# Loading a projection with two rows per partition, weights with a stride, and another order of a set-up

## The chip, the cores and the metric

The kernel runs on one core of a Trainium2 chip. A core has a matrix engine (TensorE, PE in the profile; PEld are its weight loads), a vector engine (VectorE, DVE), a scalar engine (ScalarE, ACT), GpSimd (POOL) and SyncE (SP); the last two issue the DMA transfers here, GpSimd those that change the type. The engines run side by side and wait for each other by semaphores. The metric is the device time of one execution in microseconds (us); of several executions, the median.

## The reference

Longformer attention on 8 batches of 8 heads, 576 tokens and 64 channels, followed by a two-layer projection with a "snake" activation on 4608 tokens. Cut to what matters:

```python
# attention: window of +-32 tokens, plus 8 global tokens
scores = scale * q @ k.T
attn   = softmax(where(mask, scores, -1e9))
x      = (attn @ v), laid out as 4608 tokens x 512
# projection
h   = x @ w_in                       # 512 -> 2048 features
s   = sin(alpha * h)
g   = h + s * s / (alpha + 1e-9)     # alpha: one number per feature
out = g @ w_out                      # 2048 -> 512
```

All inputs and the output are float32; the products take bfloat16.

## The kernel before

All four big tensors of the projection live in SBUF: `w_in` as 128 partitions x 4 chunks x 2048 features, `w_out` as 128 partitions x 16 feature tiles x 512, and `alphaT`, `recipT` as 128 partitions x 16, one column per feature tile (`recipT` is 1/(alpha + 1e-9)). A feature tile `nt` is 128 features that stand on the 128 partitions of PSUM after the first product. Before, tile `nt` holds the features nt*128 to nt*128 + 127 in order.

The order of work is written out by hand; each engine runs its instructions in the order in which the program calls them. `attention(b)` does one batch in four pairs of heads `hp`: `scores` (L814) into the PSUM tiles ring, zn or zd, the exponential (L822), a mask `cover` (L831); `denominators` (products with ones, L862, into zd, their logarithm L on ScalarE, L772, and the sums GD of the global tokens, L756); `inverse` (R = exp(-L), L779); and the numerators (products with v, L862, and with the global values, L878) that `normalise` (L908) multiplies by R into `xT`, the input of the projection. `gemm1(b)` then forms the 16 feature tiles: 8 products each (L1115, 4 chunks by 2 halves of the columns, each with its own weight load), a sine and a square on ScalarE (L1162, L1165) or a square on VectorE (L1167), and the sum into H (L1168). The second product, `gemm2` (L1220), is a generator: `fill(n)` takes n of its products and puts them into TensorE's queue between the attention work of the next batch. The first call, `fill(START)` with START = 7, stands at the head of the attention of batch 1; two fills of 9 products follow.

Batch 0 has a set-up of its own, `first_batch`. No second product is there yet to fill in. At its end it forms denominators, inverses and numerators of the four pairs in an order written out there, and sets `alphaT` and `recipT` in `set_recip`: a transpose of `arow` by TensorE (L710), a copy (L711), an addition (L712) and a reciprocal (L713) on VectorE. `warm` (L569) issues products with ones whose result nobody reads.

The weights come by GpSimd's queue: `load_w_in(lo, hi)` (L426) loads a range of columns, `load_w_out(gs)` (L432) a range of rows, with the cast to bfloat16 on the way. On the same queue stand the loads of q and k of batches 0 and 1 (`load_lying`, L456), the cast of v and q into DRAM for later batches (L334), and the casts of the global keys and queries (`gkq`, L717). Every DMA of that queue first waits until the eighth DMA before it has landed.

`judge` at the end checks a bound on the arguments of the sine; it sums the squares of `w_in` per feature (L1060, 16 products of one column each) into 16 columns that must agree with those of `alphaT`.

## Time and profile before

| what | value |
|---|---|
| median of 3 runs | 339.67 us (337.75 to 339.68) |
| the profiled execution | 338.49 us |
| its span, first to last instruction | 336.8 us |
| TensorE busy | 316.2 us (94%) |
| VectorE busy | 255.9 us (76%) |
| ScalarE busy | 277.1 us (82%) |
| GpSimd busy | 143.7 us (43%) |

The shares are means over stages with different limits: the set-up of batch 0 (to about 28.6 us), the first product of batch 0 (to about 51 us), then for each further batch attention with the second product of the batch before beside it, and its first product. Lines of a view give an engine, the line of the kernel, the operation, what it writes and reads, and its times. An idle time in brackets is followed by what ended it; "issue" means that the profile shows nothing that the engine waited for.

### The profile page before, as it was taken

What the parts mean: (1) busy time and instruction counts of PE and PEld (TensorE: products, weight loads), DVE (VectorE), ACT (ScalarE), POOL (GpSimd) and SP (SyncE); (2) the same over time, 40 slices, a digit from 0 to 9 for tenths busy, and PEclk for the clock granted to TensorE, in tenths of its full rate; (3) what the DMA queues carried; (4) which work ended last, traced back from release to release, by engine and by line L of the source; (5) the groups of instructions that cost most, each with busy time, mean ns of one, the idle gap of its engine ahead of it and who ended that gap; (6) DMA issues with size and microseconds to landing.
All of it is one profiled execution on the core that took longest, in us unless ns stands there. A gap on an engine that the chain in (4) does not pass through costs nothing.

```text
span 336.8 us, 11878 instructions
## 1 busy us (share of the span) xinstructions
PE 316.2 (94%) x4812; PEld 202.8 (60%) x4812; DVE 255.9 (76%) x488; ACT 277.1 (82%) x402; POOL 143.7 (43%) x296
## 2 busy tenths in 40 slices
PE   0778999999999999999999999999999999999993
PEld 0765765577556765667556755676567745665553
DVE  4885896887887788688877788778868888788930
ACT  6775888989998889988998889889898898889611
POOL 7983324349516670666355652487060000004500
PEclk9999999999999999999999999999999999999998
DMA  7999999999989998999969993899999311010232
GB/s 104 114 162 205 186 226 169 152 166 135 181 143 133 190 124 137 94 119 186 151 93 137 172 162 85 131 176 136 132 111 133 65 60 42 1 33 8 73 93 69
DMA packets 141942, 42.01 MB, mean 125 GB/s; under 512 B 126426, under 2 KB 136794, under 8 KB 141882
## 3 DMA queue, kind: packets, MB, share of 16 engines
q0 software_dynamic: 100096, 18.51, 71.1%
q1 hardware_dynamic: 41786, 22.69, 34.1%
q8 instruction: 38, 0.62, 0.8%
q14 instruction: 22, 0.18, 0.2%
HBM read 41.95 MB, written 20.77 MB: 186 GB/s over the span
## 4 chain that ended last, share of the span: by engine, by line
PE 87%; DVE 4%; ACT 3%; issue 2%; DMA 1%; POOL 1%; DVEq 0%; POOLq 0%
PE zo L1220 38%; PE zn L1115 14%; PE zr L1115 11%; PE zd L1115 10%; PE ring L814 4%; PE zd L862 4%; PE zn L862 2%; DVE H L1168 2%; DMA g0k<-in_k_dram,grow 1%; ACT sb L1162 1%; PE zn L814 1%; PE zr L862 1%; DVE recipT L712 1%; DVE s L1167 1%; PE zo L630 1%
## 5 line engine op out<-in xcount | busy, mean ns | idle before, releaser
L1220 PE MATMUL zo<-w_out,H 128*128 128x512 bf16 (+1 forms) x576 | 147.1, 377 | 0.3 <-DVE KX L637 0.3
L1115 PEld LDWEIGHTS <-w_in 128*128 128x128 bf16 x1024 | 100.1, 98 | 43.9 <-issue 8.3
L1220 PEld LDWEIGHTS <-H 128*128 128x128 bf16 x592 | 53.7, 98 | 46.2 <-issue 0.4
L1115 PE MATMUL zn<-xT,w_in 128*128 128x288 bf16 (+1 forms) x384 | 57.7, 290 | 1.6 <-DVE H L1168 1.4
L1115 PE MATMUL zr<-xT,w_in 128*128 128x288 bf16 x320 | 48.0, 288 | 0.3
L1168 DVE SCALAR_TENSOR_TENSOR H<-s,recipT,zn 128x576 bf16<-128x576 bf16 (+1 forms) x48 | 39.4, 822 | 10.4 <-ACT s L1165 6.5
L1162 ACT ACTIVATE sb<-zn,alphaT 128x576 bf16<-128x576 f32 (+1 forms) x48 | 35.7, 743 | 13.7 <-PE zn L1115 13.2
L1115 PE MATMUL zd<-xT,w_in 128*128 128x288 bf16 x320 | 46.3, 288 | 0.3 <-DVE H L1168 0.2
L822 ACT ACTIVATE E<-ring 128x720 bf16<-128x720 f32 x46 | 35.9, 780 | 8.3 <-PE ring L814 7.7
L1167 DVE TENSOR_TENSOR s<-sb 128x576 bf16<-128x576 bf16 (+1 forms) x70 | 32.6, 465 | 12.2 <-ACT sb L1162 12.0
L1165 ACT ACTIVATE s<-sb 128x576 bf16<-128x576 bf16 (+1 forms) x58 | 40.0, 689 | 1.8
L831 DVE TENSOR_TENSOR E<-E,MASKT 128x720 bf16<-128x720 bf16 x64 | 33.5, 529 | 7.6 <-ACT E L822 5.6
L1168 DVE SCALAR_TENSOR_TENSOR H<-s,recipT,zd 128x576 bf16<-128x576 bf16 (+1 forms) x40 | 32.9, 822 | 7.6 <-ACT s L1165 5.0
L1168 DVE SCALAR_TENSOR_TENSOR H<-s,recipT,zr 128x576 bf16<-128x576 bf16 (+1 forms) x40 | 32.9, 822 | 6.6 <-ACT s L1165 5.0
L344 POOL DMA_DIRECT2D kd<-in_k_dram x48 | 31.4, 657 | 10.4 <-issue 8.0
L1162 ACT ACTIVATE sb<-zd,alphaT 128x576 bf16<-128x576 f32 (+1 forms) x40 | 29.6, 740 | 5.2 <-PE zd L1115 5.1
L1162 ACT ACTIVATE sb<-zr,alphaT 128x576 bf16<-128x576 f32 (+1 forms) x40 | 29.6, 740 | 4.3 <-PE zr L1115 4.3
L1210 POOL COPY H<-H 128x11 bf16 (+1 forms) x16 | 7.2, 453 | 57.6 <-DVE H L1168 56.7
L346 POOL DMA_DIRECT2D vd<-in_v_dram x48 | 30.5, 645 | 1.7 <-issue 1.3
L346 POOL DMA_DIRECT2D qd<-in_q_dram x40 | 25.4, 635 | 6.0 <-issue 6.0
L1227 ACT COPY osb<-zo 128x512 f32<-128x512 f32 (+1 forms) x33 | 19.1, 580 | 10.6 <-PE zo L1220 7.0
L814 PEld LDWEIGHTS <-KX 64*64 64x64 bf16 x896 | 15.8, 112 | 19.4 <-issue 19.0
(171 smaller groups left out, 377.7 us busy)
## 6 DMA issues: line engine op xcount, KB each, us to landing
VF<-vd SPq DMA_DIRECT2D x14, 336.0 KB
kd<-in_k_dram POOLq DMA_DIRECT2D x48, 72.0 KB, 4.8
vd<-in_v_dram POOLq DMA_DIRECT2D x48, 72.0 KB, 4.1
qd<-in_q_dram POOLq DMA_DIRECT2D x40, 72.0 KB, 5.5
w_out<-in_moe_w_out_dram POOLq DMA_DIRECT2D x2, 1024.0 KB, 25.7
out_dram<-osb SPq DMA_DIRECT2D x7, 256.0 KB
out_dram<-osb SPq DMA_DIRECT2D x8, 224.0 KB
out_dram<-osb SPq DMA_DIRECT2D x8, 192.0 KB
```

The costliest lines, as they stand in the source:

```text
L344: nc.gpsimd.dma_start(out=dst[:, :, h], in_=src.rearrange("(i a) d -> a i d", a=KT))
L346: nc.gpsimd.dma_start(out=dst[:, h], in_=src)
L814: nc.tensor.matmul(out=z[half * D : (half + 1) * D, t, 0 : G3 * WCOL].rearrange("p (m x c) -> p m x c", x=2, c=60)[:, m % G3, :, c0:c1], l ...
L822: nc.scalar.activation(out=weights(hp, g), in_=z[:, :, 0 : G3 * WCOL], func=AF.Exp, scale=scale)
L831: nc.vector.tensor_tensor(out=Eg, in0=Eg, in1=MASKT[:, None, G3 * g : G3 * (g + 1), :].rearrange("p o m c -> p o (m c)").to_broadcast([P, ...
L862: nc.tensor.matmul(out=nd(hp, key)[t * D : (t + 1) * D, half, :, a - half * CUT : z - half * CUT], lhsT=ones[rows, 0:D] if key else values ...
L1115: nc.tensor.matmul(out=h_part, lhsT=w_in[:, c, nt * P : (nt + 1) * P], rhs=xT[:, c, lo:hi], start=(c == 0), stop=(c == CT - 1), skip_group ...
L1162: nc.scalar.activation(out=sb[:, 0:W], in_=h, func=AF.Sin, scale=alphaT[:, nt : nt + 1])
L1165: nc.scalar.activation(out=s2[:, 0:W], in_=sb[:, 0:W], func=AF.Square)
L1167: nc.vector.tensor_tensor(out=s2[:, 0:W], in0=sb[:, 0:W], in1=sb[:, 0:W], op=ALU.mult)
L1168: nc.vector.scalar_tensor_tensor(out=H2[:, nt, r0 : r0 + W], in0=s2[:, 0:W], scalar=recipT[:, nt : nt + 1], in1=h, op0=ALU.mult, op1=ALU.add,)
L1220: nc.tensor.matmul(out=ops[:, cols], lhsT=H2[:, nt, blk * P : (blk + 1) * P], rhs=w_out[:, nt, cols], start=(nt == 0), stop=(nt == NT - 1) ...
```

## The change

Four things change together.

**w_out.** It is loaded in four loads of four feature tiles instead of two of eight. Within a load each partition gets two neighbouring rows of `w_out` at a time, 1024 numbers that are contiguous in DRAM, for the two tiles 2t and 2t + 1.

**The features of a tile.** So partition p of tile 2t + j now holds feature 256 t + 2 p + j. The first product takes its weights accordingly: 128 columns of `w_in` with a step of two, by the new function `feature(nt)`. The same holds for the products of `judge` and for `general_path`, which is in the program but not run on these inputs. `alphaT` comes from an `arow` of 8 x 256 by two transposes, each of every other column.

**w_in.** The three loads are of 256, 768 and 1024 columns instead of 512, 512 and 1024, since tiles 0 and 1 now lie in the first 256 columns.

**The order in `first_batch` and in the second product of batch 0.** `inverse(0)` stands before the denominators of pair 2; `alphaT` is set right after the first numerators, a `warm` is added behind it, and the last denominators come before the second numerators; `recipT` is set after the last `normalise`. In `gemm2(0)` the first two blocks are both advanced to 12 of their 16 feature tiles, four tiles at a time in turn, where before each went to 8 at once.

On VectorE, at the end of batch 0's set-up, before (xT is the input of the projection; GD and GN are sums of the global tokens; zr, zn, zd are PSUM tiles):

```order
L908 TENSOR_TENSOR xT<-zn,R 128x576
L756 TENSOR_REDUCE GN<-zn 128x2x4
L711 COPY alphaT<-zo_125 128x16
L712 TENSOR_SCALAR recipT<-alphaT 128x16
L713 RECIPROCAL recipT<-recipT 128x16
L756 TENSOR_REDUCE GD<-zd 128x2x4
L908 TENSOR_TENSOR xT<-zr,R 128x576
L756 TENSOR_REDUCE GN<-zr 128x2x4
L908 TENSOR_TENSOR xT<-zd,R 128x576
L756 TENSOR_REDUCE GN<-zd 128x2x4
```

And the same stretch of VectorE now:

```order
L718 COPY alphaT<-zo_125 128x2x8
L768 TENSOR_REDUCE GD<-zd 128x2x4
L920 TENSOR_TENSOR xT<-zn,R 128x576
L768 TENSOR_REDUCE GN<-zn 128x2x4
L920 TENSOR_TENSOR xT<-zr,R 128x576
L768 TENSOR_REDUCE GN<-zr 128x2x4
L920 TENSOR_TENSOR xT<-zd,R 128x576
L768 TENSOR_REDUCE GN<-zd 128x2x4
L724 TENSOR_SCALAR recipT<-alphaT 128x16
L725 RECIPROCAL recipT<-recipT 128x16
```

The two instructions of recipT moved from ahead of the last GD to behind the last xT, and GD and alphaT moved ahead of the second xT.

On ScalarE, from the last exponentials of batch 0 to the first sine, before (L is the logarithm of the denominators, R their inverse):

```order
L822 ACTIVATE E<-zn 128x2x360
L772 ACTIVATE L<-zd 128x576
L779 ACTIVATE R<-L,shift 128x576 x3
L772 ACTIVATE L<-zd 128x576
L779 ACTIVATE R<-L,shift 128x576
L957 ACT_TABLE_LOAD
```

And now:

```order
L834 ACTIVATE E<-zn 128x2x360
L791 ACTIVATE R<-L,shift 128x576
L784 ACTIVATE L<-zd 128x576
L791 ACTIVATE R<-L,shift 128x576
L784 ACTIVATE L<-zd 128x576
L791 ACTIVATE R<-L,shift 128x576 x2
L972 ACT_TABLE_LOAD
```

The first inverse moved ahead of the third logarithm, and the last logarithm ahead of the third inverse.

On GpSimd's queue, from the q and k loads of batch 1 to the loads of w_out, before, with the semaphores that each waits for (DMASW0 to 7 go round, one per DMA):

```order
L426 DMA w_in<-in_moe_w_in_dram 128x4x512 [waits DMASW3_49]
L456 DMA H_97<-in_k_dram 48x4x768 [waits DMASW4_49]
L456 DMA H_97<-in_q_dram 48x4x768 [waits DMASW5_49]
L426 DMA w_in<-in_moe_w_in_dram 128x4x1024 [waits DMASW6_49]
L456 DMA H_97<-in_k_dram 48x4x768 [waits DMASW7_49]
L456 DMA H_97<-in_q_dram 48x4x768 [waits DMASW0_49]
L937 COPY seen<-VF_91 1x1 [waits DVE_49,Pool_49]
L334 DMA vd<-in_v_dram 4608x1x64 [waits DMASW1_49]
L432 DMA w_out<-in_moe_w_out_dram 128x8x512 [waits DMASW2_49]
L432 DMA w_out<-in_moe_w_out_dram 128x8x512 [waits DMASW3_49]
```

And now:

```order
L431 DMA w_in<-in_moe_w_in_dram 128x4x768 [waits DMASW3_49]
L461 DMA H_97<-in_k_dram 48x4x768 [waits DMASW4_49]
L461 DMA H_97<-in_q_dram 48x4x768 [waits DMASW5_49]
L431 DMA w_in<-in_moe_w_in_dram 128x4x1024 [waits DMASW6_49]
L461 DMA H_97<-in_k_dram 48x4x768 [waits DMASW7_49]
L461 DMA H_97<-in_q_dram 48x4x768 [waits DMASW0_49]
L949 COPY seen<-VF_91 1x1 [waits DVE_49,Pool_49]
L339 DMA vd<-in_v_dram 4608x1x64 [waits DMASW1_49]
L437 DMA w_out<-in_moe_w_out_dram 128x2x1024 [waits DMASW2_49]
L437 DMA w_out<-in_moe_w_out_dram 128x2x1024 [waits DMASW3_49]
L437 DMA w_out<-in_moe_w_out_dram 128x2x1024 [waits DMASW4_49]
L437 DMA w_out<-in_moe_w_out_dram 128x2x1024 [waits DMASW5_49]
```

The third and the fourth load of w_out now wait for the first k and q loads of batch 1 (DMASW4 and DMASW5) to have landed.

The diff, without the same edit of the weights in `general_path`:

```diff
+def feature(nt):
+
+    return slice((nt // 2) * 2 * P + nt % 2, (nt // 2 + 1) * 2 * P, 2)
...
     def load_w_in(lo, hi):
         if lo < hi:
-            cols = slice(lo * DFF // 4, hi * DFF // 4)
+            cols = slice(lo * DFF // 8, hi * DFF // 8)
...
     def load_w_out(gs):
         for g in gs:
             nc.gpsimd.dma_start(
-                out=w_out[:, 8 * g : 8 * g + 8, :],
-                in_=moe_w_out[8 * g * P : (8 * g + 8) * P, :].rearrange("(t p) n -> p t n", p=P),
+                out=w_out[:, 4 * g : 4 * g + 4, :].rearrange("p (t j) n -> p t (j n)", j=2),
+                in_=moe_w_out[4 * g * P : (4 * g + 4) * P, :].rearrange("(t p j) n -> p t (j n)", p=P, j=2),
             )
...
-    arow = setup.tile([NT, P], DT.float32, name="arow")
+    arow = setup.tile([NT // 2, 2 * P], DT.float32, name="arow")
...
-    nc.sync.dma_start(out=arow[:], in_=moe_alpha.rearrange("(t p) -> t p", p=P))
+    nc.sync.dma_start(out=arow[:], in_=moe_alpha.rearrange("(t p) -> t p", p=2 * P))
...
+    def set_alpha():
+        n = NT // 2
+        for j in range(2):
+            nc.tensor.transpose(out=zo[0][:, j * n : (j + 1) * n], in_=arow[:, j::2], identity=idf[0:n, 0:n])
+        nc.vector.tensor_copy(
+            out=alphaT[:].rearrange("p (t j) -> p j t", j=2),
+            in_=zo[0][:, 0:NT].rearrange("p (j t) -> p j t", j=2),
+        )
+
     def set_recip():
-        nc.tensor.transpose(out=zo[0][:, 0:NT], in_=arow[:], identity=idf[0:NT, 0:NT])
-        nc.vector.tensor_copy(out=alphaT[:], in_=zo[0][:, 0:NT])
         nc.vector.tensor_scalar(out=recipT[:], in0=alphaT[:], scalar1=1e-9, scalar2=None, op0=ALU.add)
         nc.vector.reciprocal(out=recipT[:], in_=recipT[:])
...
-                    load_w_in(1, 2)
+                    load_w_in(1, 4)
...
-                            load_w_in(2, 4)
+                            load_w_in(4, 8)
...
-                    load_w_out((0, 1))
+                    load_w_out(range(4))
                 beside(hp)
                 for g in range(2 * (hp > 0)):
                     cover(hp, g)
+                if hp == last:
+                    inverse(0)
                 if hp:
                     denominators(hp - 1)
             release_ring()
-            for hp in range(2):
-                inverse(hp)
-                first_numerators(hp)
-            set_recip()
-            inverse(last - 1)
+            inverse(1)
+            first_numerators(0)
+            set_alpha()
+            warm(zo[1], 1)
             denominators(last)
-            first_numerators(last - 1)
+            inverse(2)
+            first_numerators(1)
+            first_numerators(2)
             warm(zo[1], 1)
             products(last, 0)
...
             normalise(last)
+            set_recip()
...
-                out=zn[:, 0, nt : nt + 1], lhsT=W2[:, nt * P : (nt + 1) * P], rhs=ones[:, 0:1],
+                out=zn[:, 0, nt : nt + 1], lhsT=W2[:, feature(nt)], rhs=ones[:, 0:1],
...
-                        out=h_part, lhsT=w_in[:, c, nt * P : (nt + 1) * P], rhs=xT[:, c, lo:hi],
+                        out=h_part, lhsT=w_in[:, c, feature(nt)], rhs=xT[:, c, lo:hi],
...
-        ahead = {0: NT // 2, B - 1: SOON}.get(b, 0)
-        for blk in (lo, lo + 1):
-            yield from products(blk, bank(blk), range(ahead), full)
+        ahead = {0: 3 * NT // 4, B - 1: SOON}.get(b, 0)
+        step = NT // 4 if b == 0 else NT
+        for nt in range(0, ahead, step):
+            for blk in (lo, lo + 1):
+                yield from products(blk, bank(blk), range(nt, min(nt + step, ahead)), full)
```

More of the change, by code (lines that the diff above doesn't have):

```diff
@@ L201, in general_path @@
                         nc.tensor.matmul(
-                            out=hg[:, e, 0:HALF], lhsT=w_in[:, c, nt * P : (nt + 1) * P],
+                            out=hg[:, e, 0:HALF], lhsT=w_in[:, c, feature(nt)],
                             rhs=xT[:, c, e * HALF : (e + 1) * HALF],
```

## The prediction

> **What bounds the kernel now.** I read the busy time of each engine by stretches first, then the chain of work that ended last from 18 to 36 us, then the timeline around it. The first view gives a stretch, its length, and the busy time of TensorE, its weight loads, VectorE, ScalarE and GpSimd, each with its instruction count; below it stands one row of the timeline (start, length, engine, line, what it does, idle time before it):
>
> ```profile
> 0.00:50.00 50.00, 35.54 (x914) 27.21 (x915) 37.01 (x91) 37.02 (x55) 29.52 (x52) 1.00 1.23 165
> 50.00:310.00 260.00, 259.06 (x3746) 163.52 (x3746) 206.49 (x374) 230.32 (x337) 108.07 (x235) 1.00 1.11 122
> ...
> 6.51 0.24 PE L630 MATMUL zn<-identb,H 48*64 48x48 bf16 x1 [6.51 <-DMA H<-in_k_dram]
> ```
>
> TensorE is busy 259.06 of 260 us in the middle: there nothing but its own work counts, and a time won at the front arrives at the end undiminished. In the first 50 us it idles 50 - 35.54 = 14.5 us. All that a new order of the set-up can win lies in there. Of that, 6.51 us is the wait for the first load, which this change leaves alone. The chain (start, length, engine and line) shows what set the pace just before the product with w_in begins:
>
> ```profile
> 24.23 2.14 DVE recipT L712
> ...
> 26.40 0.25 DVE recipT L713
> 26.65 0.09 DVE GD L756
> ...
> 28.80 1.44 PE zn L1115 x6
> 30.24 0.93 PE zr L1115 x6
> ```
>
> recipT, 16 columns wide, takes 2.14 us, and behind it on VectorE stands the reduction GD, which must read zd before TensorE may write the last numerators into it. From the start of L712 to the GD piece are 26.65 - 24.23 = 2.42 us. The timeline tells why so small an instruction is so long:
>
> ```profile
> 23.79 2.16 POOL L334 DMA_DIRECT2D vd<-in_v_dram  x1
> 24.23 2.13 DVE L712 TENSOR_SCALAR recipT<-alphaT 128x16 f32<-128x16 f32 x1
> 24.38 0.51 PE L862 MATMUL zd<-E,ones 56*64 56x120 bf16 x16 [1.02 <-issue]
> 24.94 0.65 ACT L772 ACTIVATE L<-zd 128x576 f32<-128x576 f32 x1 [0.94 <-PE zd L862]
> 25.48 1.34 POOL L432 DMA_DIRECT2D w_out<-in_moe_w_out_dram  x1
> ```
>
> GpSimd is issuing the v load from 23.79 to 25.95, and L712 ends at 26.36. The reciprocal L713 of the same 16 columns takes 0.25 beside the next issue. I read it as one instruction held off by an issue that it happened to meet, with a work of its own of about 0.25.
>
> **1. The set-up of batch 0.** recipT moves behind the last normalise, alphaT ahead of the last denominators, and those ahead of the second numerators. Taking away L712 alone would not give 2.42: GD needs L, which ends at 24.94 + 0.65 = 25.59, so TensorE's zd could start near 25.7 in place of 26.78, 1.07 earlier. Moving the denominators forward puts L before that, and what is late next is TensorE's own queue. Its pieces:
>
> ```profile
> 20.24 0.79 PE L862 MATMUL zd<-E,ones 56*64 56x88 bf16 x28
> 20.86 0.77 PE L862 MATMUL zr<-E,VF 56*64 56x88 bf16 x28
> 21.68 0.78 PE L862 MATMUL zn<-E,VF 56*64 56x88 bf16 x28
> 22.66 0.28 PE L710 MATMUL zo<-idf,arow 16*128 16x16 f32 x1
> 24.67 0.82 PE L862 MATMUL zr<-E,VF 56*64 56x88 bf16 x28
> 25.69 0.61 PE L569 MATMUL zo<-ones 128*128 128x512 bf16 x1
> 26.78 0.79 PE L862 MATMUL zd<-E,VF 56*64 56x88 bf16 x28 [0.48 <-DVE GD L756]
> 27.77 1.03 PE L569 MATMUL zo<-ones 128*128 128x512 bf16 x2
> 28.60 1.65 PE L1115 MATMUL zn<-xT,w_in 128*128 128x288 bf16 x6
> ```
>
> From start to start: denominators 20.86 - 20.24 = 0.62, second numerators 22.66 - 21.68 = 0.98, third 25.69 - 24.67 = 1.02, last 27.77 - 26.78 = 0.99, the closing two warm-ups 28.60 - 27.77 = 0.83; and by their lengths, alpha 0.28 and one warm-up 0.61. The new queue behind the first numerators, from 21.68 on, is alpha 0.28, an added warm-up 0.61, denominators 0.62, numerators 0.98 and 1.02, warm-up 0.61, numerators 0.99, two warm-ups 0.83: 5.94 us, to 27.62. Before it was 28.60. So 1.0 is won if TensorE never waits. It waited 1.02 for "issue" at 24.38, with no producer late; if that comes back in full, nothing is left. I take 0.7, nearer the upper end, because the pieces taken by their lengths count a tail that overlaps the next one.
>
> The first six products take 1.44 and the next six 0.93, against 8 in 1.14 and 2 in 0.41 later (rows below). At the later pace, (1.14 - 0.41) / 6 = 0.122 each, the twelve would cost 1.46, so they lose 1.44 + 0.93 - 1.46 = 0.9. The profile prints a granted clock of 1.00 there (last but two of the columns above), yet the rate says slow. A queue with fewer holes may end that sooner; 0 to 0.9, and I take 0.4. The Trainium skill's page "TensorE: Matmul & The Clock Gate", section "What's actually happening", says the clock is halved until the array was busy for a window of some 3.4 us; the twelve products agree in kind.
>
> recipT now meets GpSimd's later issues: at worst it lasts 2.13 again, but its first reader is L1168, which stood 32.81 - 28.60 = 4.2 us behind the first product; hidden. If a w_out issue meets a square of the activation instead, that square can stretch:
>
> ```profile
> 31.02 0.41 PE L1115 MATMUL zn<-xT,w_in 128*128 128x288 bf16 x2
> ...
> 32.81 0.81 DVE L1168 SCALAR_TENSOR_TENSOR H<-s,recipT,zn 128x576 bf16<-128x576 bf16 x1
> ...
> L1167 DVE TENSOR_TENSOR s<-sb x8: 448/451/996, 32.2 to 52.1; 128x576 bf16<-128x576 bf16 x8
> 33.67 1.14 PE L1115 MATMUL zn<-xT,w_in 128*128 128x288 bf16 x8 [1.03 <-DVE H L1168]
> ```
>
> The squares (minimum, median, maximum in ns) show 996 - 451 = 0.5 in such a meeting, and TensorE does wait for VectorE in that stage. 0 to +0.5, taken at +0.1.
>
> **2. w_in in pieces of 256, 768 and 1024 columns.** The issues of the first two loads, and from issue to landing the shortest, median and longest of the three, which are the first, second and third in order:
>
> ```profile
> 16.50 0.87 POOL L426 DMA_DIRECT2D w_in<-in_moe_w_in_dram  x1
> ...
> 19.88 0.76 POOL L426 DMA_DIRECT2D w_in<-in_moe_w_in_dram  x1
> ...
> DMA to landing us min/median/max: 6.3/7.5/14.1
> ```
>
> The first landed at 16.5 + 6.3 = 22.8, the second at 19.88 + 7.5 = 27.4. The same bytes in the same queue end at 27.4; if the small piece saves nothing, the second takes 1.5 times 27.4 - 22.8 = 4.6, to 29.7. It is first needed by feature tile 2 (at 31.50 in the next fence), 2.9 after the first product, so at 27.6 + 2.9 = 30.5 or later. Nothing, with 0.8 us of cover; beyond that each us costs one.
>
> **3. Every other column as weights.** This touches 1024 loads, all on the engine that bounds the kernel:
>
> ```profile
> L1115 PEld LDWEIGHTS <-w_in 128*128 128x128 bf16 x1024 | 100.1, 98 | 43.9 <-issue 8.3
> 31.50 1.14 PE L1115 MATMUL zd<-xT,w_in 128*128 128x288 bf16 x8
> 323.87 0.60 PEld L1060 LDWEIGHTS <-VF 128*128 128x128 bf16 x16
> ```
>
> No load of before has a stride, so this is bounded. Where nothing hides them, 16 loads pass in 0.60: (0.60 - 0.098) / 15 = 33 ns apart. Beside a product of 288 columns, which repeats every 122 ns, a load could become 3.6 times slower unseen. Lower end 0 (the products' own rate excludes a gain); upper end, if 98 ns doubles and is paid whole, (196 - 122) x 1024 = 76 us. I take 0: 33 is the rate that matters, and doubling it gives 66. At the end of the kernel the 16 loads of L1060 are strided too and have no cover: 0 to 16 x (98 - 33) = 1.0 us, taken as 0, since the doubled rate costs 0.5 and may lie beside other waits.
>
> The Trainium skill, same page, section "Weight-path perf modes", says that the fast load reads two bf16 as one 32-bit word, which a stride of two would spoil, while allowing strides. By the formula of its section "LDWEIGHTS (loading the stationary operand)" the plain load is an estimated 128 / 1.2 = 107 ns: still below 122, the sum unchanged, and 16 x (107 - 33) = 1.2 us more at L1060. No run shows a strided load yet.
>
> **4. w_out in four loads and the product's order.** Rows for the old loads and their first uses:
>
> ```profile
> DMA to landing us min/median/max: 22.9/25.7/28.6
> 27.63 0.89 POOL L432 DMA_DIRECT2D w_out<-in_moe_w_out_dram  x1 [0.80 <-DMA w_in<-in_moe_w_in_dram]
> 51.34 1.67 PE L1220 MATMUL zo<-w_out,H 128*128 128x512 bf16 x7 [0.25 <-DVE KX L637]
> 53.39 2.12 PE L1220 MATMUL zo<-w_out,H 128*128 128x512 bf16 x9
> 56.23 1.02 PE L1220 MATMUL zo<-w_out,H 128*128 128x512 bf16 x4
> ```
>
> The halves landed at 25.48 + 22.9 = 48.4 and 27.63 + 28.6 = 56.2, and the 17th product, the first to need the second half, started at 56.23: no slack. With the old order a front 1.0 earlier would wait there. Now products 1 to 16 need quarters 0 and 1, the 17th quarter 2, the 25th quarter 3. At the old rate quarter 2 lands at (48.4 + 56.2) / 2 = 52.3 against a need near 55.2, quarter 3 at 56.2 against 55.2 + 8 x 0.22 = 57.0 (one product is (2.12 - 1.02) / 5 = 0.22). Covered by 0.8, before any gain from larger pieces. The loads wait for the eighth load before them on GpSimd's queue, so the third and fourth are issued later, behind lying loads of batch 1, but the first half landed only at 48.4, so the queue has work ahead of them and the later issue costs nothing. Behind them on GpSimd stand the gkq casts, first read by feature tile 12, and the q load of batch 2. Four issues at about 0.6 cost what two cost now (1.34 + 0.89). Block 0 now ends at product 28 and its bank is written again at product 33, four products of 0.22 on where it was eight; ScalarE's copy must fit in between:
>
> ```profile
> L1227 ACT COPY osb<-zo 128x512 f32<-128x512 f32 (+1 forms) x33 | 19.1, 580 | 10.6 <-PE zo L1220 7.0
> ```
>
> 0.88 us of products hold a copy of 0.58; if the copy waits behind an exponential, 0 to 0.6, taken as 0 since attention work of TensorE also lies between.
>
> **Sum.** -0.7 - 0.4 + 0.1 = -1.0. The profiled execution took 338.49 us (span 336.8 and 1.69 around it): 337.5. The runs have a median of 339.67, 1.2 above it, and 1.0 off that is 338.7. I put the forecast between the two, at 338.1.
>
> **The rivals.** *Nothing won*: TensorE's issue gaps return whole and the slow first products stay: the issue gap eats the 1.0 and the loss of 0.9 remains, so the time is that of before, 339.1 by the same middle. For it: 1.02 at 24.38 has no producer behind it. Against: 2.42 of the chain goes. 0.20.
>
> *More won*: no gap, and the twelve products at full rate: 1.0 + 0.9 = 1.9, and another 1.03, the wait for H at 33.67, if the product's first tiles run smoother: 339.1 - 1.9 = 337.2 down to 336.1. For it: 14.5 - 6.5 = 8 us of idle time in the front. Against: a wait for H is one for VectorE, whose work there is not less. 0.22.
>
> *w_out late*: the four loads each pay a fixed time in turn. If each of the four takes the 0.9 of an issue more, the last lands 3.6 later, at 59.8; TensorE waits 59.8 - 57.0 = 2.8, and the time is 338.1 + 2.8 = 340.9. Against it stand the twelve v loads:
>
> ```profile
> L392 POOL DMA_DIRECT2D VF<-in_v_dram x12: 647/680/704, 9.0 to 15.9; - x12
> DMA to landing us min/median/max: 2.9/3.5/3.9
> ```
>
> They are issued 0.63 apart and land 3.5 after, so fixed times overlap. The page "DMA: Bandwidth & Descriptors", section "Bandwidth", of the Trainium skill advises loads of at least 1 MiB, against this split; the rows speak for overlap. 0.07.
>
> *Strided weights seen*: the side of slower. If a strided load takes four times 33, 134 ns, each of 1024 products waits 12: +12.3, 350.4. It decides from 122 ns per load on. Nothing in the profile shows a stride, the 3.6-fold cover speaks against it. 0.06.
>
> **How the numbers follow.** The forecast keeps 0.45. Within 1% of 339.67 is 336.3 to 343.1, about what a measurement of this kernel can tell from no change. Faster by more: over half of "more won", with medians that scatter by 1 around it, 0.13, and a tenth of the forecast's own share by the same scatter, 0.04: 0.17. Slower by more: the strided weights and a far worse w_out, 0.07. The same: 0.76. The range, 335.6 to 341.0, reaches from the best of more won less half of the scatter of 1.2 to late w_out; outside lie the strided weights and the tails, under 0.2.
>
> **What would show it.** Right: recipT behind the last xT and off the chain, the first L1115 product at 27.6 to 28.4, strided loads of w_in at the same 122 ns per product, no TensorE wait at products 17 and 25. Wrong: 8 products longer than 1.14, idle time before the w_out products put down to a DMA, or a wait of feature tile 2 for w_in.

## The result, and the profile after

The changed kernel takes 348.36 us (median of 4 runs, 346.95 to 349.27) against 338.99 us for the kernel before (4 runs, 337.75 to 339.68). The ratio is 1.0268, with a 95% interval of 1.0233 to 1.0304: slower by 9.4 us. The profiled span grew from 336.8 to 345.9 us, by 9.1.

The table by stretches of the kernel after, with the columns of the first fence of the prediction, shows in which stretch it went. The last three columns are the granted clock, the DMA share and GB/s:

```profile
0.00:50.00 50.00, 29.45 (x740) 21.52 (x741) 26.37 (x78) 29.12 (x43) 28.82 (x51) 0.90 1.19 160
50.00:310.00 260.00, 258.52 (x3867) 164.34 (x3866) 207.50 (x375) 230.14 (x340) 107.14 (x230) 1.00 1.09 123
```

TensorE is busy 29.45 us of the first 50, where it was 35.54. The middle is as full as before (258.52 of 260). So the loss lies in the front, and the timeline of the kernel after, TensorE alone, has it in one row:

```profile
27.91 0.56 PE L1131 MATMUL zn<-xT,w_in 128*128 128x288 bf16 x2
37.20 1.12 PE L1131 MATMUL zn<-xT,w_in 128*128 128x288 bf16 x4 [8.73 <-DMA w_in<-in_moe_w_in_dram]
38.12 1.64 PE L1131 MATMUL zr<-xT,w_in 128*128 128x288 bf16 x6
39.55 0.68 PE L1131 MATMUL zn<-xT,w_in 128*128 128x288 bf16 x2
40.03 0.68 PE L1131 MATMUL zr<-xT,w_in 128*128 128x288 bf16 x2
40.52 1.80 PE L1131 MATMUL zd<-xT,w_in 128*128 128x288 bf16 x8
42.49 1.14 PE L1131 MATMUL zn<-xT,w_in 128*128 128x288 bf16 x8 [0.17 <-DVE H L1184]
...
60.14 1.67 PE L1236 MATMUL zo<-w_out,H 128*128 128x512 bf16 x7 [0.25 <-DVE KX L642]
```

The first product with w_in starts at 27.91, which is 0.69 earlier than before (28.60). Two products run, both halves of the first of four chunks of feature tile 0, and the third waits 8.73 us for a load of w_in. Which load it is, the chain of waits after 18 us and the group of the three issues of w_in tell (first and last start; shortest, median and longest time to landing):

```profile
21.78 15.29 DMA w_in<-in_moe_w_in_dram
```

```profile
L431 POOL DMA_DIRECT2D w_in<-in_moe_w_in_dram x3: 757/763/857, 16.5 to 21.8; - x3
...
DMA to landing us min/median/max: 4.6/7.4/15.3
```

The load that ends the wait is the last one, issued at 21.78 and landed at 21.78 + 15.3 = 37.1. It holds feature tiles 8 to 15. The product that waited reads columns of tile 0. Those came with the first load, at 16.5 + 4.6 = 21.1; even the second load had landed by 19.88 + 7.4 = 27.3, before the product with w_in began.

The price is more than the wait. Stretches of the kernel after, around it:

```profile
27.00:38.00 11.00, 2.27 (x16) 0.99 (x9) 1.24 (x4) 0.75 (x1) 3.34 (x5) 0.71 1.17 207
38.00:41.00 3.00, 3.00 (x15) 1.79 (x14) 0.00 (x0) 0.72 (x2) 2.22 (x1) 0.50 2.41 156
41.00:42.00 1.00, 1.00 (x6) 0.68 (x5) 0.83 (x2) 0.97 (x3) 0.00 (x0) 0.57 2.17 187
42.00:50.00 8.00, 7.69 (x148) 5.57 (x147) 6.99 (x12) 7.15 (x12) 0.00 (x0) 1.00 1.13 220
```

The granted clock falls during the wait, is 0.50 from 38 to 41 us and 1.00 again from 42 us on. The third product starts at 37.20, where before it started at about 28.60 + 2 x 1.44 / 6 = 29.1: 8.1 late. The 17th product starts at 40.52, where it was 31.50: 9.0 late, so the slower pace of the products between them adds 0.9. The next eight run longer, but beside them the wait for H ahead of the 25th shrinks from 1.03 to 0.17, and the 25th stands at 42.49 for 33.67, 8.8 late. The first product with w_out is 60.14 - 51.34 = 8.8 late, and the end 9.1.

The rest of the change did in the profile of after what it was meant to do: recipT is off the chain, 0.18 us long where it took 2.13, and the strided weights cost the same as the contiguous ones, with cover and without. The page's group of weight loads, and rows of the timeline for VectorE and for the weight loads at the end:

```profile
L1131 PEld LDWEIGHTS <-w_in 128*128 128x128 bf16 x1024 | 100.7, 99 | 52.9 <-issue 16.6
```

```profile
28.10 0.18 DVE L724 TENSOR_SCALAR recipT<-alphaT 128x16 f32<-128x16 f32 x1
```

```profile
332.82 0.60 PEld L1076 LDWEIGHTS <-VF 128*128 128x128 bf16 x16
```

### The profile page after: what moved, and what is told of

The parts are those of the page before. It is cut to its first block, busy times and chain, and to the rows that moved or that the text cites. A ratio compares the mean times of both kernels' runs of the same rounds, so it can differ in the third digit from the quotient of the medians.

```text
span 345.9 us, 11886 instructions
## 1 busy us (share of the span) xinstructions
PE 318.5 (92%) x4814; PEld 203.4 (59%) x4814; DVE 254.1 (73%) x488; ACT 276.8 (80%) x402; POOL 144.2 (42%) x298
## 4 chain that ended last, share of the span: by engine, by line
PE 83%; DMA 6%; DVE 4%; ACT 3%; POOL 2%; issue 2%; DVEq 0%; POOLq 0%
PE zo L1236 37%; PE zn L1131 13%; PE zr L1131 11%; PE zd L1131 10%; DMA w_in<-in_moe_w_in_dram 4%; PE ring L826 4%; PE zd L874 3%; PE zn L874 2%; DVE H L1184 2%; DMA H<-in_q_dram 1%; ACT sb L1178 1%; DVE s L1183 1%; POOL H L461 1%; ACT s L1181 1%; PE zr L874 1%
## 5 line engine op out<-in xcount | busy, mean ns | idle before, releaser
L1131 PE MATMUL zr<-xT,w_in 128*128 128x288 bf16 x320 | 48.7, 292 | 0.3
L1183 DVE TENSOR_TENSOR s<-sb 128x576 bf16<-128x576 bf16 (+1 forms) x70 | 32.6, 465 | 21.3 <-ACT sb L1178 21.1
## 6 DMA issues: line engine op xcount, KB each, us to landing
w_out<-in_moe_w_out_dram POOLq DMA_DIRECT2D x4, 512.0 KB, 21.4
```

The costliest lines, as they stand in the source:

```text
L1131: nc.tensor.matmul(out=h_part, lhsT=w_in[:, c, feature(nt)], rhs=xT[:, c, lo:hi], start=(c == 0), stop=(c == CT - 1), skip_group_check=True,)
L1183: nc.vector.tensor_tensor(out=s2[:, 0:W], in0=sb[:, 0:W], in1=sb[:, 0:W], op=ALU.mult)
```

## The experiments

### Why the third product waits

The list of the built program's instructions, TensorE's alone, shows which queue of loads each weight load is made to wait for. DMASW2, 3 and 6 count the first, second and third load of w_in. Before (rows 1139, 1203, 1459: feature tiles 0, 4 and 8) and after (rows 1142 and 1146: both in tile 0):

```
1139 L1115 LDWEIGHTS w_in [waits DMASW2_49]
1203 L1115 LDWEIGHTS w_in [waits DMASW3_49]
1459 L1115 LDWEIGHTS w_in [waits DMASW6_49]

1142 L1131 LDWEIGHTS w_in [waits DMASW2_49]
1146 L1131 LDWEIGHTS w_in [waits DMASW6_49,DMASW3_49]
```

So the wait is in the program, not in the speed of a load. The theory: w_in is one tile of four chunks of 2048 columns, and each load writes its columns in all four, so loads interleave. A weight load with a step of two is taken to touch whatever lies between, if it comes behind the start of a load's region and ahead of its end. Chunk 0 of tile 0 lies ahead of the later loads' regions; chunk 1 lies inside them. A contiguous read is made to wait only for the load of its own columns, as the list of the kernel before shows.

**Strided features alone.** The kernel before with the new `feature(nt)` for the weights of w_in and W2, and two rows of w_out per partition in the two old loads; the loads of w_in (512, 512, 1024 columns), the set-up and the order of products are the old ones.

```
-  lhsT=w_in[:, c, nt * P : (nt + 1) * P]
+  lhsT=w_in[:, c, feature(nt)]
...
-  out=w_out[:, 8 * g : 8 * g + 8, :],
+  out=w_out[:, 8 * g : 8 * g + 8, :].rearrange("p (t j) n -> p t (j n)", j=2),
```

> The kernel before with nothing but the strided features: weights of every other column, w_out in its two old loads with two rows per partition, alpha to match; old order of the set-up, old pieces of w_in (512, 512, 1024). Theory 1: TensorE waits in the third product from about 29 us until the third load of w_in lands (36 to 37 us), 7 to 8 us, and the time is 346 to 349. Theory 2 (late landing of the small first piece and the larger second): no wait, since the old pieces are back, 338.5 to 340. Theory 3 (slow strided weights): slower by an amount spread over all batches, with the same products per us in no stage.

Measured: 346.7 us (4 runs), ratio 1.0214 [1.0173, 1.0255]. Its timeline, TensorE alone:

```profile
29.05 0.69 PE L1125 MATMUL zn<-xT,w_in 128*128 128x288 bf16 x2
36.26 1.12 PE L1125 MATMUL zn<-xT,w_in 128*128 128x288 bf16 x4 [6.53 <-DMA w_in<-in_moe_w_in_dram]
```

The same product waits, without the new pieces of w_in, the new set-up or the new order. The stride alone is enough for the wait, and for 7.7 of the 9.4 us (346.7 against 338.97 for the kernel before in the same round). The wait ends 0.9 earlier here than in the changed kernel (36.26 for 37.20); the rest of the difference was not broken down.

**All but the stride.** The kernel before with the new order of the set-up, w_out in four loads (one row per partition) and the new order of the products; weights contiguous, and w_in in its old three pieces. The edits of first_batch() are those of the change.

```
-  load_w_out((0, 1))
+  load_w_out(range(4))
-  ahead = {0: NT // 2, B - 1: SOON}.get(b, 0)
+  ahead = {0: 3 * NT // 4, B - 1: SOON}.get(b, 0)
...
```

> The kernel before with the new set-up order, w_out in four loads (of contiguous feature tiles, one row per partition) and the new order of the second product of batch 0; weights contiguous, w_in in its old pieces. Theory 1: no wait for w_in; the first product of w_in starts about 0.7 us earlier and the end with it, 0.5 to 1.5 us below the kernel before. Rival (the new order costs by itself): not below the kernel before.

Measured: 338.96 us (12 runs), ratio 0.9988 [0.9964, 1.0013]. There is no wait for w_in, and nothing of the 9 us is left. What it should have won is not there either. Its first product with w_in starts at 28.53, only 0.07 earlier than before and not the 0.7 that was expected, behind a gap in the front that is put down to issue:

```profile
24.96 0.35 PE L864 MATMUL zn<-E,VF 56*64 56x120 bf16 x9 [1.34 <-issue]
```

Such gaps, and where the rest of the gain goes, are taken up below.

**A tile for each load.** The whole change, strided weights and all, with w_in in three tiles, one per load; w_of() takes the tile that holds nt and counts feature() from its start.

```
+  parts = [(0, 2), (2, 8), (8, NT)]
+  w_ins = [const.tile([P, CT, (z - a) * P], DT.bfloat16, name=f"w_in{i}") for i, (a, z) in enumerate(parts)]
-  lhsT=w_in[:, c, feature(nt)]
+  lhsT=w_of(c, nt)
```

> The changed kernel with w_in kept in three tensors, one per load (256, 768 and 1024 columns); weights are still every other column, loads, orders and w_out as changed. Theory 1 (the wait is one of bookkeeping: with a step of two in the read, weights of the second chunk of the first tile are taken to overlap the two later loads): the idle 8.7 us before the third product of w_in is gone, first products run at 27.9 us on, time about 0.7 to 1.7 us below the kernel before, so 337 to 338.5. Theory 2 (the first 256 columns really are not there, because the loads land late): the wait stays, 347 to 349. Theory 3 (strided weights slow the products): 8 products still take over 1.14 us somewhere and the time stays near 348.

Measured: 338.46 us (12 runs), ratio 0.9974 [0.9951, 0.9997]. Each tile is waited for at its own first feature tile. The stride stays, the wait goes.

**One tile, loads not interleaved.** Three tiles differ from one in two ways, so the next kernel keeps one tile and puts each load's columns in a stretch of their own.

```
+  w_in = const.tile([P, CT * DFF], DT.bfloat16, name="w_in")
+  w_ins = [w_in[:, a * P * CT : z * P * CT].rearrange("p (c n) -> p c n", c=CT) for a, z in parts]
```

> The change with w_in still one tile, but the columns of each load lie in a stretch of their own, one behind the other, in place of between those of the other loads in each of the four chunks. Weights keep their stride of two. Theory (a strided read is taken to touch whatever lies between, and loads that interleave by chunks lie there): the wait list now has load 2 at feature tile 2 and load 3 at feature tile 8; no wait for w_in over 0.3 us, median 338.5, ratio 0.997. Rival (a tile that several loads write is waited for as a whole): the third product waits 6 to 9 us and the time is 346 to 348.

Measured: 338.29 us (10 runs), ratio 0.9967 [0.995, 0.9984]. In its list of instructions the three waits stand at feature tiles 0, 2 and 8. So it is neither the tile nor the stride by itself, but a strided read among interleaved loads. The weights' group on its page and TensorE's timeline:

```profile
L1138 PEld LDWEIGHTS <-w_in 128*128 128x128 bf16 x1024 | 99.8, 98 | 43.5 <-issue 8.2
```

```profile
27.67 1.04 PE L1138 MATMUL zn<-xT,w_in 128*128 128x288 bf16 x6
28.55 0.90 PE L1138 MATMUL zr<-xT,w_in 128*128 128x288 bf16 x6
...
29.77 1.14 PE L1138 MATMUL zd<-xT,w_in 128*128 128x288 bf16 x8
```

With no stall, 1024 strided loads take 98 ns each, eight products 1.14 us, and the first twelve products 29.28 - 27.67 = 1.61 us, where before they took 31.02 - 28.60 = 2.42.

**The third load earlier.** The change with the third load of w_in issued right behind the second, about 1 us earlier.

```
   load_w_in(1, 4)
+  load_w_in(4, 8)
-  if hps == early:
-      load_w_in(4, 8)
```

> The changed kernel with the third load of w_in issued right behind the second, ahead of the q and k loads of batch 1 that stood between. Theory 1: the wait ends with the landing of the third load, which comes 2 to 3.5 us earlier (37.1 to about 34), and the time falls by about as much, to 345 to 346.5, unless the q and k loads are then late for the transposes. Theory 2 (the wait is for the second load): no shorter, 348. Theory 3: no change, 348.

Measured: 345.26 us (4 runs), ratio 1.0168 [1.0127, 1.021], span 343.9. Its timeline:

```profile
26.44 0.41 PE L1130 MATMUL zn<-xT,w_in 128*128 128x288 bf16 x2
35.21 1.12 PE L1130 MATMUL zn<-xT,w_in 128*128 128x288 bf16 x4 [8.36 <-DMA w_in<-in_moe_w_in_dram]
```

The wait ends 37.20 - 35.21 = 2.0 earlier and the span is 2.0 shorter; by the medians the time falls by 3.1 (348.36 to 345.26). The first product with w_in starts 1.5 earlier, yet the wait is only 0.4 shorter (8.36 for 8.73): its end goes with the landing of the third load, which is issued at 20.7 for 21.8, and not with the start of the product.

### Where the front's gain goes

**The set-up's order alone.** The kernel before with the new first_batch() and the split of set_recip() into set_alpha() and set_recip(), as in the change's diff; loads and products as before.

> The kernel before with only batch 0's set-up in the new order; loads, weights and the order of the products with w_out as before. Theory 1 (no slack at the 17th product with w_out, whose load landed at 56.2): the front wins 0.5 to 1.3 us, and the 17th product then waits for the load by the same amount; median as before, ratio 0.999 to 1.001. Theory 2 (TensorE's gaps put down to issue eat it before): the first product with w_in starts at 28.2 or later, and no wait for w_out appears; ratio 1.000. Rival: the gain is kept, 338.0, ratio 0.997.

Measured: 338.88 us (12 runs), ratio 0.999 [0.997, 1.001]. The first product with w_in starts at 27.82 (0.78 earlier), the first with w_out at 49.88 (1.46 earlier), and then its timeline has:

```profile
56.30 2.10 PE L1226 MATMUL zo<-w_out,H 128*128 128x512 bf16 x9 [1.48 <-DMA w_out<-in_moe_w_out_dram]
```

The 17th product stands at 56.30, where it was 56.23. All that the set-up won is given back to the second half of w_out.

**w_out alone.** The kernel before with four loads, one row per partition, and the new order of the products; the set-up as before.

> The kernel before with only w_out in four loads of four feature tiles and the products' new order (rows as before, weights contiguous, old set-up). Theory: the quarters land at or before 56.2, the 25th product stands at 57.5 or later, nothing waits: ratio 0.999 to 1.001. Rival 1 (four loads are later than two): the 25th product waits over 0.3 us for w_out, ratio 1.001 to 1.003. Rival 2 (the kernel before was held back by its second half): ratio 0.997.

Measured: 339.07 us (12 runs), ratio 0.9999 [0.9981, 1.0017]. No product waits for w_out. Alone it is worth nothing in the time; that its use is to let an earlier front through is argued here, not tested by itself.

The profile of this run shows one thing more. Its set-up is the old one, and yet its first product with w_in starts 1.15 earlier than in the kernel before. The addition L712 takes 0.17 us here, for 2.13, and the last numerators start 1.07 earlier (25.71 for 26.78), which is what the prediction put on L712 alone:

```profile
23.74 2.16 POOL L334 DMA_DIRECT2D vd<-in_v_dram  x1
23.91 0.17 DVE L712 TENSOR_SCALAR recipT<-alphaT 128x16 f32<-128x16 f32 x1
...
27.45 1.65 PE L1115 MATMUL zn<-xT,w_in 128*128 128x288 bf16 x6
```

The v load was being issued beside it here too. So the long L712 is not a fixed cost of the old order, an issue that runs beside it is not enough to cause it, and what held it off in the profile of before stays open.

With both (the kernel above with all but the stride, and those with w_in apart) the 17th product no longer waits. But the profile of the three tiles shows two waits right behind it:

```profile
57.06 0.38 PE L1242 MATMUL zo<-w_out,H 128*128 128x512 bf16 x1 [0.74 <-DMA w_out<-in_moe_w_out_dram]
...
60.27 0.21 PE L879 MATMUL zd<-E,ones 56*64 56x32 bf16 x4 [0.46 <-issue]
```

The first is the 25th product, which needs the last quarter of w_out. At the first product with w_out this kernel was 51.34 - 49.56 = 1.78 ahead. Some 40 products on, its row and that of the kernel before:

```profile
63.98 1.68 PE L1242 MATMUL zo<-w_out,H 128*128 128x512 bf16 x7
```

```profile
64.23 1.68 PE L1220 MATMUL zo<-w_out,H 128*128 128x512 bf16 x7
```

Of the 1.78 there is 0.25 left.

**The 25th product later.** The three tiles, with that product moved to the next place where products fill in.

```
-  SECOND_FIRST = (9, 9, 5, 7)
+  SECOND_FIRST = (9, 8, 6, 7)
```

> The change with w_in in three tiles, and 8 in place of 9 products of w_out placed at the second fill, 6 in place of 5 at the fourth, so that the 25th, the first to need the last quarter of w_out, stands one fill later. Theory: the 0.74 us that this product waited for the load were the price that ate what the front had won; without it the median lies 0.5 to 0.7 below that of the three tiles alone, near 337.8 (ratio 0.996), and no wait for w_out is left. Rival: attention is late there anyway (VectorE's E, ScalarE's exponentials), so the time moves into waits for ring and E behind it: median as with the three tiles alone, 338.4, ratio 0.997 to 0.998.

Measured: 338.47 us (12 runs), ratio 0.9985 [0.9964, 1.0005]. The wait for w_out is gone and the time is not lower: the rival was right that another wait takes its place, but not about which. It is again one put down to issue, inside the 28 denominators of L879, and the same gap stands in the one-tile kernel:

```profile
59.73 0.21 PE L879 MATMUL zd<-E,ones 56*64 56x32 bf16 x3 [1.16 <-issue]
```

```profile
60.62 0.21 PE L880 MATMUL zd<-E,ones 56*64 56x32 bf16 x4 [1.67 <-issue]
```

Moving one product from before to behind the gap left 3 matmuls behind it in place of 4. The gap thus stands at a fixed count of TensorE's instructions and not at what stands there, which speaks for the loading of these instructions; the last section has the counts.

**Eight pairs of instructions more.** The one-tile kernel with eight small pairs of a weight load and a product at the start of TensorE's queue, while it idles for the first load.

```
+  for _ in range(8):
+      nc.tensor.matmul(out=zo[1][:, 0:32], lhsT=ones[:], rhs=ones[:, 0:32], ...)
```

> The one-tile kernel without the wait for w_in, plus eight pairs of a weight load and a 32-column product at the very start of TensorE's queue, where it idles for the first load for over 6 us. Nothing else moves. It asks what the idle time of 1.67 us is that the one-tile profile puts down to issue at 58.95 to 60.62, behind 24 of the 28 denominators. Theory 1 (TensorE waits for its own next block of instructions, which lies at a fixed count): the gap falls eight pairs earlier in the program, behind 16 of the 28, 12 left, and ends again 2.3 to 2.5 us after the start of an instruction packet of the queue q8; the gaps of the front move by eight pairs too. Theory 2 (the last denominators wait for VectorE's mask of E, which ended just before, at 60.34): the gap stays behind 24 of the 28, 4 left. Time by either: as the one-tile kernel within 0.5 us, 338.0 to 338.8.

Measured: 337.4 us (10 runs), ratio 0.9958 [0.993, 0.9985]. In the front the gap moved as instruction loading says, by eight matmuls. The one-tile kernel and this one, TensorE's timeline:

```profile
15.26 0.38 PE L880 MATMUL zd<-E,ones 56*64 56x120 bf16 x9 [0.90 <-issue]
```

```profile
15.16 0.58 PE L882 MATMUL zd<-E,ones 56*64 56x120 bf16 x17 [0.53 <-issue]
...
56.91 0.38 PE L1245 MATMUL zo<-w_out,H 128*128 128x512 bf16 x1 [1.24 <-DMA w_out<-in_moe_w_out_dram]
58.31 1.03 PE L1245 MATMUL zo<-w_out,H 128*128 128x512 bf16 x4 [0.16 <-issue]
```

Nine were left behind the gap, now seventeen. Near 60 us the expectation missed: no gap falls among the denominators at all (the 0.16 at 58.31 stands where only four of five products have a record). The DMA view suggests a reason: the packet of instructions that starts at 58.14 in the one-tile kernel starts at 55.89 here, while TensorE, held by the wait of the 25th product for w_out until 56.91, comes to that place at about 59.7. The gaps elsewhere end 2.3 to 3.0 us behind a packet's start; that would be 58.9 at the latest, so the instructions were probably there in time. The scores before 64 us start at 62.84, where the one-tile kernel has 63.73.

**Both.** That kernel with the 25th product later, by the same edit of SECOND_FIRST as above.

> The one-tile kernel with the eight early pairs, and the 25th product of w_out one fill later (8 in place of 9 at the second fill, 6 in place of 5 at the fourth), since it waited 1.24 us for the last quarter of w_out there. Theory 1 (that wait is the last loss near 60 us): no wait for w_out, gap for instructions under 0.5 us, median 336.4 to 337.0, ratio 0.992 to 0.995. Theory 2 (another wait takes its place, for the next block of instructions as in the three-tile kernel with the later product, 1.16 us): ratio 0.995 to 0.998.

Measured: 337.87 us (12 runs), ratio 0.9974 [0.9946, 1.0002]. The ratio is that of theory 2, but the wait that takes the place is not the one that it named. The wait for w_out goes and one for a transfer of batch 1 comes:

```profile
56.65 0.23 PE L882 MATMUL zn<-E,VF 56*64 56x88 bf16 x2 [0.46 <-DMA VF<-VGb]
57.11 0.49 PE L882 MATMUL zn<-E,VF 56*64 56x88 bf16 x26 [0.23 <-DMA VF<-VGb]
```

These kernels with w_in apart lie between 0.9958 and 0.9985, and their intervals overlap. That the one-tile kernel, with or without the eight pairs, is faster than the kernel before is shown (by 0.3 and 0.4%, with intervals that leave out 1); which of them is the best is not.

## Why the prediction was wrong

The prediction was 338.1 us, within 335.6 to 341.0; measured were 348.36. It said no change, and it is slower.

- **Step 2, w_in in pieces: the step that failed.** "Nothing, with 0.8 us of cover" asked when each load lands and which feature tile needs its data. The landings were no later than I worked with, 21.1 and 27.3 for 22.8 and 27.4 to 29.7. But a product starts when all the loads that it is made to wait for have landed, not when its own data is there. The old kernel's waits stood at tiles 0, 4 and 8, so the two questions had the same answer, and I took them for one. In the changed kernel all three waits stand in tile 0. The sign that I named, "a wait of feature tile 2 for w_in", came at the third product, still in tile 0, and it waited for the load of tiles 8 to 15. The price that I gave, one us for each us beyond the cover, held for the wait (8.1 of delay at the third product); the slower pace behind it, 0.9, was not in it.
- **Step 3, the strided weights**, was put at 0 with bounds up to 76 us, and 0 it is, for TensorE: 98 ns and 1.14 us per eight products in the one-tile kernel, and 16 uncovered loads in 0.60 us, as before. That a stride of two would spoil the fast load was my own inference, and no run shows it. The plain load that the Trainium skill's page "TensorE: Matmul & The Clock Gate" led me to estimate at 107 ns (section "LDWEIGHTS (loading the stationary operand)") is not seen where nothing covers the loads: by that estimate 16 would take 16 x 107 ns = 1.7 us, and the row shows 0.60. But I looked for the cost of a stride only in the engine that reads with it. It was the stride among interleaved loads that cost 9 us, through the waits. The rival "strided weights seen" had the right part of the change and the wrong mechanism, and its sign, products longer than 1.14, came for another reason (the halved pace behind the wait).
- **Step 1, the set-up**, came out near, in part by luck. The front won 0.69 in the changed kernel (taken at 0.7), 0.78 alone; recipT left the chain and took 0.18. But each is one profile, and the start of the first product with w_in varies by more than this gain: 28.60, 29.05 and 27.45 with the old set-up (before, strided features alone, w_out alone), 27.07 to 28.53 in the kernels with the new one (but for the third load earlier, 26.44). With the old set-up L712 is long in two of the three profiles (2.13 and 1.98) and takes 0.17 in the other, so the 2.42 of the chain that spoke against "nothing won" is not lost in every execution. The slow first twelve products, from 2.42 before, took 2.00 with three tiles, 1.61 with one tile and 1.47 with all but the stride: 0.4 to 0.95 won, about the stated 0 to 0.9, of which I took 0.4.
- **Step 4, w_out**, held in the loads, but its cover for the 25th product did not last. The first and last quarter landed at 25.48 + 20.4 = 45.9 and 32.03 + 23.7 = 55.7 in the changed kernel (median 21.4). That the 17th product had no slack was shown by the set-up's order alone: 1.48 of wait. The cover of 0.8 for the 25th product set a need at 57.0, with a front 1.0 earlier, against a landing at 56.2. With three tiles the front was 1.78 ahead, so the product was ready at 56.3, and the wait for its quarter ended at 57.06: 0.7 earlier and 0.9 later than worked out, and so a wait of 0.74. With the eight pairs it was 1.24; in the one-tile kernel the product did not wait.
- **The sum of the other steps**, -1.0, is near what two kernels without the wait for w_in show: ratio 0.9967 is -1.1 us, 0.9974 is -0.9. That is partly luck: they reach it with more won at the front (1.7 to 1.8 at the first product with w_out) and more given back near 57 and 60 us. The kernel with all but the stride shows -0.4 (0.9988), with an interval that holds 1.
- **The rival "nothing won"** feared TensorE's gaps put down to issue, and these are real: the kernel with all but the stride has one of 1.34 us at 24.96, at the same count of instructions as the 1.02 at 24.38 before, and its front wins 0.07; its timeline has another of 1.32 us at 61.09.

## What to carry to other kernels

When a change alters the form of a read (a stride, another view), look up in the built program which loads each reader now waits for; when its data lands is only half of the question. If a tile is filled by several loads and read with a step, give each load a stretch of its own, or a tile of its own: here that turned 1.0268 into 0.9967. And a cover worked out for one forecast start is to be worked out again for the largest gain that the same change may bring ahead of it.

## What the runs showed of the hardware

**TensorE's gaps put down to issue follow its instruction packets.** The DMA view lists a queue q8 of kind instruction. Narrowing its window until the packet falls out gives each packet's start to within 0.05 us; the one-tile kernel's window of 58.00 to 59.20 has one (packets, MB, share of 16 engines):

```profile
q8 instruction: 1, 0.02, 4.6%
```

| kernel | packet starts | gap on TensorE ends | later by |
|---|---|---|---|
| before | 16.89 | 19.26 | 2.4 |
| before | 22.07 | 24.38 | 2.3 |
| three tiles | 57.92 | 60.27 | 2.4 |
| three tiles, 25th later | 57.32 | 59.73 | 2.4 |
| one tile | 58.14 | 60.62 | 2.5 |
| all but the stride | 58.77 | 61.09 | 2.3 |
| eight pairs more | 12.14 | 15.16 | 3.0 |

One row of the table, from the timeline of the kernel before:

```profile
19.26 0.51 PE L814 MATMUL zn<-QX,KX 64*64 64x120 bf16 x14 [0.51 <-issue]
```

The gap of 1.02 at 24.38, on which the rival "nothing won" rested, is one of these. The gaps end 2.3 to 3.0 us behind a packet's start, and eight pairs ahead move one by eight pairs. In the built programs' lists, with TensorE's semaphore instructions counted, and the weight load that the profile shows with each float32 transpose, the first instruction behind such a gap has number 447, 703, 959 or 2239. This holds in the kernel before, the one-tile kernel, the one with eight pairs and the one with all but the stride, wherever they have the gap. The numbers lie 256 apart, the last five times 256, and the page of the kernel before has 38 packets for TensorE's some 9,640 instructions, 254 for each. The Trainium skill, page "Runtime: NRT & Kernel Launch", section "Instruction fetch mechanics", says that instructions come in blocks of 16 KiB by the sequencer's own DMA queue and that crossing a block is mostly hidden. The packets' 0.02 MB agree with the size. Mostly hidden agrees too: in the kernel before, three of the 38 leave a gap put down to issue (0.68, 0.51 and 1.02 us). In the front and near 60 us, a crossing that shows cost 0.34 to 1.67 us in these runs. Why a packet starts when it does was not tried. In the kernel before, a packet starts at 57.99 too, but TensorE reaches the place at about 60.6, late enough not to wait.

**The pace after a wait.** Behind 8.73 us of idling, two products took 40.03 - 39.55 = 0.48 us in the changed kernel, where two took 31.26 - 31.02 = 0.24 before. The granted clock is printed as 0.50 there and as 1.00 from 42 us on, so the slow stretch lasted from 37.20 to about 41.9, some 4.7 us. The Trainium skill, page "TensorE: Matmul & The Clock Gate", section "What's actually happening", states a clock halved until the array was busy for a free-running window of some 3.4 us; the factor of two agrees, and a stretch between one window and two agrees as well. The printed clock alone is not a safe sign of it: with the strided features alone, the products behind the wait of 6.53 us are as slow (39.09 - 38.61 = 0.48), and the clock is printed as 1.00 throughout:

```profile
38.61 0.69 PE L1125 MATMUL zn<-xT,w_in 128*128 128x288 bf16 x2
39.09 0.69 PE L1125 MATMUL zr<-xT,w_in 128*128 128x288 bf16 x2
```

```profile
36.00:40.00 4.00, 3.74 (x16) 2.42 (x17) 0.00 (x0) 0.66 (x2) 2.43 (x2) 1.00 2.02 172
```

The first twelve products before are such a case as well: 0.24 us each at first, with a printed clock of 1.00.
